# A decode attention kernel's SBUF places moved: first keys in the values' place, w1 and the second keys beside it, later query weights loaded mid-run

## The chip, the cores and the metric

The kernel runs on one core of a Trainium2 chip. The metric is the device time of one execution in microseconds. A difference of 0.3% (4 us) is about the least that can be told from no change here.

## What is computed

One decode step for eight sequences: a layer norm, then in parallel grouped-query attention over a cache of 8192 positions (32 query heads, 8 key/value heads of 128) and a dense layer with Mish; both are added to the input.

```python
xn = layernorm(x)                       # 8 x 512
q = (xn @ wq)                           # 32 heads x 128
scores = einsum("bhqd,bhkd->bhqk", q, repeat(k_cache, 4)) * 128 ** -0.5
o = einsum("bhqk,bhkd->bhqd", softmax(scores), repeat(v_cache, 4))
h = xn @ w1 + b1                        # 8 x 1792
act = h * tanh(softplus(h))
return x + o @ wo + act @ w2
```

All is float32. The caches are 268 MB each, so nearly all of the 561 MB that the kernel reads is keys and values, each read once.

## The kernel before

**Units.** The work is cut into 32 units, j = 0 to 31. Unit j holds batch b = j % 8 and the pair of key/value heads m = j // 8. Its keys are one load of 8.39 MB (128 partitions x 16384 floats, `ROW`) and its values another. wq is cut into four pairs of 2.10 MB (16 KB in each partition), one for each m; w1 is 3.67 MB, b1 is small.

**Places.** One SBUF tile, `kv`, takes every large load, as 2.5 x `ROW` columns. Even keys stand at 0, odd keys at `ROW // 2`: two units of keys share a half place. Values stand at 1.5 x `ROW` (`V_AT`). Before the loop the values' place holds three pairs of wq, then w1 (over the first two), b1 and the fourth pair; its spare part serves as scratch for Mish. x, its centred copy and its squares stand in the keys' place, at `ROW`.

**Queues.** The schedule is by hand: each engine executes its instructions in the order in which the program emits them, and the framework adds the waits. All large loads are issued by SyncE (`load_unit` L118, `load_pair` L111, w1 L425), in program order, each after its place has been read; x and b1 are issued by ScalarE. A load waits only for accesses to the columns that it overwrites.

**Before the loop.** x, three pairs of wq and keys 0 are issued. VectorE makes constants and the layer norm; `tr` (through its view `wide`) receives sixteen copies of the identity (L198). `project(m)` (L204 to L241) multiplies the normed x by the pair's weights (L209), copies it out on ScalarE (L217), transposes it through a matmul (L220), scales it into `qT` on VectorE (L228), and spreads it over the partitions with sixteen 128x128 selections taken from `wide` (L232, two halves, each copied by ScalarE into `qr`, L239). Each of these matmuls shows as two instructions in the profile. Projections 0, 1 and 2 run ahead of unit 0, projection 3 inside it.

**A unit.** `key_weights(j)` (L250, VectorE) expands the queries into block weights `wk`, of which there is one buffer. `scores` (L267, TensorE) multiplies them with the keys in two halves (`part`); the half that the next keys will overwrite is read first, and right after it SyncE issues the next keys. `softmax` (L279 to L300) is a short chain over VectorE, TensorE and ScalarE. `values(j - 1)` (L329) then reads the values of the unit before, after which SyncE issues the values of unit j into that place. `key_weights(j + 1)` follows on VectorE, and `turn(j)` transposes the probabilities: matmuls into X (L306), transposes into `tr` (L311) and reductions into `pt8` (L317), on VectorE. `merge(j - 1)` ends the unit. In unit 0 there are no values to read; in their place stand `mish` (L353 to L390, mostly a chain of VectorE steps that ends in the transpose into `aT`) and `project(3)`.

**The tail.** After the last unit the rows of wo and w2 are loaded into places that have come free, and the two output products are formed and added (L399, L411, L489).

Of the kernel before, what the change touches and what calls it, by code (L numbers as in the profile page):

```python
# [8 lines left out]
F32 = mybir.dt.float32  # L9
# [4 lines left out]
P = 128  # L14
B = 8
D = 512
HKV = 8
REP = 4
DH = 128
# [5 lines left out]
G = 4  # L25
NH = 2
TG = SK // (NH * G) // P
BW = 1024
CC = D // P
FG = F // G  # L30
FT = 4
FP = FG // FT
Q = P // G


NP = HKV // 2
NB = 2 * NH * G
ROW = NB * P * BW // P
DI = ROW // BW
# [11 lines left out]
W2R = 7  # L51


K_AT = (0, ROW // 2)
V_AT = ROW + ROW // 2
PLACES = V_AT + ROW


@with_exitstack
def kernel(  # L60
# [18 lines left out]
    ctx.enter_context(tc.manual_schedule())  # L79

    kv = const.tile([P, PLACES], F32, name="kv")

    S = psum.tile([P, 512], F32, name="s")
    X = psum.tile([P, 4, 512], F32, name="x4")
# [12 lines left out]
    gsel = const.tile([G, G, B], F32, name="gsel")  # L97
    xn4 = const.tile([P, CC, B], F32, name="xn4")
    xnT = const.tile([P, CC, B], F32, name="xnT")
    qr = const.tile([P, NP, DI, H2 * B], F32, name="qr")  # L100
    xres = const.tile([P, P], F32, name="xres")
    oT = const.tile([P, NP, H2, B], F32, name="oT")
    aT = const.tile([P, 2 * W2R, Q], F32, name="aT")
    pt8 = const.tile([P, HALF, PL * TL, H2], F32, name="pt8")
    tr = const.tile([P, PL * TL, 32], F32, name="tr")

    def load_pair(src, m, at):

        t = kv[:, at : at + 4096]
        rows = src.rearrange("j p f -> (j p f)").rearrange("(m p f) -> m p f", m=NP, p=P)  # L110
        nc.sync.dma_start(t, rows[m])  # L111
        return t

    def load_unit(src, j, at):
        m, b = divmod(j, B)
        lo = (b * HKV + 2 * m) * NH * G
        t = kv[:, at : at + ROW]
        nc.sync.dma_start(  # L118
            t,
            src[lo : lo + NB].rearrange("j p f -> (j p f)").rearrange("(p f) -> p f", p=P),  # L120
        )
        return t

    def load_k(j):
        return load_unit(kT, j, K_AT[j % 2])


    low = kv[:B, ROW : ROW + 3 * D]
    x_sb, xc, sq = (low[:, i * D : (i + 1) * D] for i in range(3))
    nc.scalar.dma_start(x_sb, x)  # L130
    wq_t = [load_pair(wq, m, V_AT + 4096 * m) for m in range(NP - 1)]
    k_t = {0: load_k(0)}


    make_identity(nc, ident)
# [51 lines left out]
    for g in range(G):  # L187
# [5 lines left out]
            stop=True,  # L193
        )
    nc.vector.tensor_copy(xres, M[:, 256:384])

    wide = tr.rearrange("p y c -> p (y c)")
    nc.vector.tensor_copy(  # L198
        wide.rearrange("p (o d) -> p o d", o=NB),
        ident.rearrange("p (o d) -> p o d", o=1).to_broadcast([P, NB, P]),  # L200
    )


    def project(m):  # L204

        w = wq_t[m].rearrange("p (c f) -> p c f", c=CC)
        for d in range(2):
            for c in range(CC):
                nc.tensor.matmul(  # L209
                    H[Q * c : Q * c + B, :],  # L210
                    xn4[:, c, :],
                    w[:, c, d * 512 : (d + 1) * 512],
                    start=True,
                    stop=True,
                )
            qp = work.tile([P, 512], F32, name="e")
            nc.scalar.copy(qp, H)  # L217
            for h in range(REP):
                at = 192 + (d * REP + h) * B
                nc.tensor.matmul(  # L220
                    M[:, at : at + B],
                    qp[:, h * DH : (h + 1) * DH],
                    bsel[:, :B],
                    start=True,
                    stop=True,
                )
        qT = work.tile([P, H2 * B], F32, name="qT")
        nc.vector.tensor_scalar_mul(qT, M[:, 192 : 192 + H2 * B], DH**-0.5)  # L228

        for half in range(2):  # L230
            for k in range(8):
                nc.tensor.matmul(  # L232
                    X[:, half, k * 64 : (k + 1) * 64],
                    wide[:, half * 8 + k :: DI],
                    qT,
                    start=True,
                    stop=True,
                )
            nc.scalar.copy(  # L239
                qr[:, m, half * 8 : (half + 1) * 8].rearrange("p i c -> p (i c)"), X[:, half]  # L240
            )  # L241

    WK = {}

    def key_weights(j):
        m, b = divmod(j, B)
        w = WK[j] = work.tile([P, DI, 2, NH * G, REP], F32, name="wk", bufs=1)
        q = qr[:, m].rearrange("p i (d o h b) -> p i d o h b", d=2, o=1, b=B)[..., b]
        for d in range(2):
            nc.vector.tensor_mul(  # L250
                w[:, :, d],
                q[:, :, d].to_broadcast([P, DI, NH * G, REP]),
                mask[:, d * NH * G : (d + 1) * NH * G]
                .rearrange("p (o k r) -> p o k r", o=1, r=1)
                .to_broadcast([P, DI, NH * G, REP]),
            )
# [20 lines left out]
    def softmax(j):  # L277
        nm = work.tile([P, 1], F32, name="nm")
        nc.vector.tensor_reduce(nm, S, axis=AX.X, op=ALU.max, negate=True)  # L279
        nc.tensor.transpose(M[:1, 0:P], nm, ident)  # L280
        nr = work.tile([1, 2, REP], F32, name="nr")
        row = M[:1, 0:P].rearrange("p (c d k h) -> p d h c k", c=2, d=2, h=REP)
        for d in range(2):
            nc.vector.tensor_reduce(nr[:, d], row[:, d], axis=AX.XY, op=ALU.min)
        nx = work.tile([1, 2, 2, NH * G, REP], F32, name="nx")
        for c in range(2):
            nc.vector.tensor_copy(  # L287
                nx[:, c],
                nr.rearrange("p d (o h) -> p d o h", o=1).to_broadcast([1, 2, NH * G, REP]),
            )  # L290
        nc.tensor.transpose(  # L291
            M[:, 128:129], nx.rearrange("p c d k h -> p (c d k h)"), ident[:1, :1]
        )
        nmx = work.tile([P, 1], F32, name="nmx")
        nc.vector.tensor_copy(nmx, M[:, 128:129])  # L295
        e = E[j] = work.tile([P, 512], F32, name="e")
        l = work.tile([P, 1], F32, name="l")
        nc.scalar.activation(e, S, AF.Exp, bias=nmx, accum_out=l)  # L298
        lsel = work.tile([P, H2], F32, name="lsel")
        nc.vector.tensor_scalar(lsel, rsel, l, None, op0=ALU.mult)  # L300
        return lsel
# [42 lines left out]
    def merge(j, os):  # L344
        m, b = divmod(j, B)
        nc.tensor.matmul(M[:, 168 : 168 + H2], os, hsel, start=True, stop=True)  # L346
        nc.vector.tensor_mul(oT[:, m, :, b], M[:, 168 : 168 + H2], RT.pop(j))


    def mish(w1_t, b1_sb, flat):  # L350
# [33 lines left out]
        for e in range(2):  # L384
# [2 lines left out]
                h[:, half * e : half * (e + 1)].rearrange("p (a l i) -> p a l i", a=2, i=W2R),  # L387
                t1[:, half * e : half * (e + 1)].rearrange("p (a l i) -> p a l i", a=2, i=W2R),
            )
        nc.vector.transpose(aT.rearrange("p j q -> p (j q)"), act)  # L390


    A = X[:, 0]
# [13 lines left out]
    def down(lo, hi, w):  # L407
        for j in range(2 * lo, 2 * hi):
            for g in range(G):
                at = (j - 2 * lo) * D + g * P  # L410
                nc.tensor.matmul(  # L411
                    H[Q * g : Q * g + B, :P],
                    aT[:, j, :B],
                    w[:, at : at + P],
                    start=(j == 0),
                    stop=(j == 2 * W2R - 1),
                )


    for m in range(NP - 1):  # L420
        project(m)
        if m == 0:
            key_weights(0)
    w1_t = kv[:, V_AT : V_AT + 7168].rearrange("p (j f) -> p j f", j=2 * CC)
    nc.sync.dma_start(w1_t, w1.rearrange("j p f -> p j f"))  # L425
    b1_sb = kv[:G, V_AT + 12288 - FG : V_AT + 12288]
    nc.scalar.dma_start(b1_sb, b1.rearrange("(g f) -> g f", g=G))
    wq_t.append(load_pair(wq, NP - 1, V_AT + 4096 * (NP - 1)))

    v_t = {}  # L430
    for j in range(UNITS):

        k = k_t.pop(j)
        scores(j, k, j % 2 == 1, 0)
        if j + 1 < UNITS:
            k_t[j + 1] = load_k(j + 1)
        else:
            v_t[j] = load_unit(v, j, 0)
        scores(j, k, j % 2 == 0, 1)
        WK.pop(j)  # L440
        lsel = softmax(j)
        os = None
        if j > 0:
            os = values(j - 1, v_t.pop(j - 1))
        else:
            mish(w1_t, b1_sb, kv[:, V_AT + 8192 : V_AT + 12288 - FG])
            project(NP - 1)
        if j + 1 < UNITS:
            v_t[j] = load_unit(v, j, V_AT)
            key_weights(j + 1)  # L450
        turn(j, lsel)
        if j > 0:
            merge(j - 1, os)


    w_o = [kv[:, V_AT + 4096 * m : V_AT + 4096 * (m + 1)] for m in range(NP)]
    for m in range(NP):
        nc.sync.dma_start(
            w_o[m].rearrange("p (u f) -> p u f", u=4),
# [3 lines left out]
    w2_t = []  # L463
    parts = ((0, 4), (4, 6), (6, 7))
    for lo, hi in parts:
        t = kv[:, ROW + lo * BW : ROW + hi * BW]
        nc.sync.dma_start(t, w2_rows[:, lo * BW : hi * BW])  # L467
        w2_t.append(t)

# [15 lines left out]
        )  # L485
    for p, t in zip(parts[1:], w2_t[1:]):
        down(*p, t)
    res = const.tile([P, P], F32, name="res")
    nc.vector.tensor_add(res, H[:, :P], xres)  # L489
    nc.sync.dma_start(out, res)  # L490

# [37 lines left out]
```

## Time and profile before

| | |
|---|---|
| time, median of 3 runs | 1344.5 us (1343.58 to 1347.8) |
| the profiled execution's own time | 1344.25 us |
| its span, first to last instruction | 1342.5 us |
| instructions | 11144 |
| TensorE busy, share of span | 999.7 us, 74% |
| VectorE busy | 508.4 us, 38% |
| ScalarE busy | 40.2 us, 3% |
| bytes moved, mean rate | 561.79 MB, 418 GB/s |
| mean granted TensorE clock | 0.875 |

In the profile's lines PE is TensorE (PEld its weight loads), DVE is VectorE, ACT is ScalarE, SP is SyncE; a q behind the name (SPq) is that engine's issuing of transfers. L267 is line 267 of the kernel before. `out<-in` names what an instruction writes and reads; x64 counts instructions merged into a row; a bracket tells how long the engine stood idle before it and what ended that. A row of the stages view holds the stage, its length, then for PE, PEld, DVE, ACT and POOL the busy time and the count, then the granted clock, the DMA share and GB/s. DMA shares in the slices are tenths.

### The profile page before, as it was taken

The page shows a single profiled execution, that of the slowest core. Times are in us where ns is not written, and L with a number is a line of the kernel's source. Part 1 is how long each engine was busy: PE and PEld are TensorE (multiplying, and loading weights), DVE is VectorE, ACT ScalarE, POOL GpSimd, SP SyncE. Part 2 cuts the span into 40 slices and gives each one's busy share as a digit, 9 for nine tenths or more (in the row PEclk, how much of TensorE's full clock was granted, in tenths as well). Part 3 has the DMA queues.
Part 4 walks back from the last instruction along what each step waited for, and adds up shares of the span by engine and source line. Part 5 has one row for each costly group of instructions (what it writes and reads, how often), then busy time and mean ns, then how long its engine had stood idle before and what let it go on. Part 6 is the DMA issues. An engine that isn't in the chain of part 4 may idle for free.

```text
span 1342.5 us, 11144 instructions
## 1 busy us (share of the span) xinstructions
PE 999.7 (74%) x5040; PEld 350.6 (26%) x5040; DVE 508.4 (38%) x724; ACT 40.2 (3%) x88; POOL 2.2 (0%) x9
## 2 busy tenths in 40 slices
PE   6879878677876776787676777777766887687676
PEld 4633222222222222222222222222222222222222
DVE  2043444443324444333344443244444224444431
ACT  1110000000000000000000000000000000000000
POOL 0000000000000000000000000000000000000000
PEclk9988888889988888888888789878888978887898
DMA  9569999999999999999999999999999999999997
GB/s 407 204 282 405 436 432 418 436 438 429 432 436 435 434 426 434 432 434 438 436 426 430 434 426 434 436 436 436 432 432 436 421 438 438 426 434 430 434 417 319
DMA packets 13591, 561.79 MB, mean 418 GB/s; under 512 B 1244, under 2 KB 1376, under 8 KB 4584
## 3 DMA queue, kind: packets, MB, share of 16 engines
q1 hardware_dynamic: 13520, 561.06, 97.1%
q8 instruction: 39, 0.64, 0.2%
q14 instruction: 8, 0.07, 0.0%
q10 hardware_dynamic: 24, 0.02, 0.0%
HBM read 561.01 MB, written 0.07 MB: 418 GB/s over the span
## 4 chain that ended last, share of the span: by engine, by line
DMA 70%; PE 26%; DVE 2%; SPq 2%; ACT 1%; issue 0%; ACTq 0%
DMA kv<-in_v 68%; PE o L329 19%; PE x L232 2%; PE s L267 2%; DMA kv<-in_w 2%; SPq L467 1%; PE m L220 1%; PE h L209 1%; PE x L306 0%; ACT e L217 0%; PE h L358 0%; ACT qr L239 0%; DVE kv L380 0%; DVE nm L279 0%; ACT L172 0%
## 5 line engine op out<-in xcount | busy, mean ns | idle before, releaser
L267 PE MATMUL s<-kv,wk 128*64 128x512 f32 x2048 | 512.0, 664 | 199.9 <-DMA kv<-in_kT 199.9
L329 PE MATMUL o<-kv,pt 128*32 128x512 f32 x2048 | 262.1, 670 | 49.7 <-DMA kv<-in_v 40.1
L267 PEld LDWEIGHTS s<-kv,wk 128*64 128x64 f32 x2048 | 157.2, 153 | 529.4 <-issue 326.6
L317 DVE TENSOR_REDUCE pt<-tr 64x512 f32<-64x2048 f32 x64 | 241.3, 3771 | 1.6
L279 DVE TENSOR_REDUCE nm<-s 128x1 f32<-128x512 f32 x32 | 22.1, 692 | 419.7 <-PE s L267 419.7
L329 PEld LDWEIGHTS o<-kv,pt 128*32 128x32 f32 x2048 | 68.9, 121 | 216.5 <-issue 164.1
L306 PE MATMUL x<-e,perm 128*128 128x512 f32 x256 | 121.3, 617 | 0.8 <-ACT qr L239 0.8
L337 DVE TENSOR_SCALAR os<-o,isel 128x128 f32<-128x128 f32 x32 | 11.2, 351 | 262.7 <-PE o L329 262.7
L311 DVE STREAM_TRANSPOSE tr<-x 128x512 f32<-128x512 f32 x128 | 78.6, 670 | 0.0
L306 PEld LDWEIGHTS x<-e,perm 128*128 128x128 f32 x256 | 47.1, 194 | 74.5 <-issue 74.5
L250 DVE TENSOR_TENSOR wk<-qr,mask 128x512 f32<-128x512 f32 x64 | 62.9, 1025 | 8.9 <-ACT qr L239 8.9
L298 ACT ACTIVATE e<-s,nmx 128x512 f32<-128x512 f32 x32 | 22.0, 687 | 1160.6 <-DVE nmx L295 1160.6
L232 PE MATMUL x<-qT,tr 128*128 128x64 f32 x128 | 29.9, 426 | 8.5 <-DVE qT L228 5.8
L339 DVE SCALAR_TENSOR_TENSOR os<-o,isel,os 128x128 f32<-128x128 f32 x96 | 33.7, 351 | 3.4
L232 PEld LDWEIGHTS x<-qT,tr 128*128 128x128 f32 x128 | 28.4, 309 | 9.6 <-DVE qT L228 6.1
L280 PE MATMUL m<-ident,nm 128*1 128x128 f32 x32 | 8.6, 270 | 25.5 <-DVE nm L279 25.5
L291 PE MATMUL m<-ident,nx 1*128 1x1 f32 x32 | 7.0, 217 | 24.2 <-DVE nx L287 24.2
L346 PE MATMUL m<-hsel,os 128*128 128x8 f32 x64 | 12.4, 266 | 9.3 <-DVE rt L309 9.3
L300 DVE TENSOR_SCALAR lsel<-rsel,l 128x8 f32<-128x8 f32 x32 | 7.4, 231 | 30.5 <-ACT e L298 30.5
L220 PE MATMUL m<-bsel,e 128*128 128x8 f32 x64 | 13.8, 344 | 6.0 <-ACT e L217 6.0
L220 PEld LDWEIGHTS m<-bsel,e 128*128 128x128 f32 x64 | 13.0, 301 | 18.5 <-ACT e L217 18.5
L280 PEld LDWEIGHTS m<-ident,nm 128*1 128x1 f32 x32 | 2.5, 79 | 53.7 <-DVE nm L279 53.7
(87 smaller groups left out, 156.7 us busy)
## 6 DMA issues: line engine op xcount, KB each, us to landing
kv<-in_wq SPq DMA_DIRECT2D x4, 2048.0 KB, 14.8
kv<-in_wo SPq DMA_DIRECT2D x4, 2048.0 KB, 29.3
kv<-in_w SPq DMA_DIRECT2D x1, 3584.0 KB, 13.5
kv<-in_w SPq DMA_DIRECT2D x1, 2048.0 KB, 37.1
kv<-in_w SPq DMA_DIRECT2D x1, 1024.0 KB, 20.7
kv<-in_kT SPq DMA_DIRECT2D x32, 29.4
kv<-in_v SPq DMA_DIRECT2D x32, 30.1
kv<-in_w SPq DMA_DIRECT2D x1, 512.0 KB
```

Source lines behind the costliest of these rows:

```text
L209: nc.tensor.matmul(H[Q * c : Q * c + B, :], xn4[:, c, :], w[:, c, d * 512 : (d + 1) * 512], start=True, stop=True,)
L220: nc.tensor.matmul(M[:, at : at + B], qp[:, h * DH : (h + 1) * DH], bsel[:, :B], start=True, stop=True,)
L232: nc.tensor.matmul(X[:, half, k * 64 : (k + 1) * 64], wide[:, half * 8 + k :: DI], qT, start=True, stop=True,)
L250: nc.vector.tensor_mul(w[:, :, d], q[:, :, d].to_broadcast([P, DI, NH * G, REP]), mask[:, d * NH * G : (d + 1) * NH * G] .rearrange("p (o ...
L267: nc.tensor.matmul(S[64 * c : 64 * (c + 1), :], w[:, i].rearrange("p d k h -> p (d k h)"), kk[:, i, c, :], start=(part == 0 and n == 0), s ...
L279: nc.vector.tensor_reduce(nm, S, axis=AX.X, op=ALU.max, negate=True)
L298: nc.scalar.activation(e, S, AF.Exp, bias=nmx, accum_out=l)
L306: nc.tensor.matmul(X[:, g], perm[:, g], e, start=True, stop=True)
L311: nc.vector.transpose(tr.rearrange("p (l t) c -> p t l c", t=TL)[:, tl], X.rearrange("p g (t q l) -> p t l g q", t=TL, q=PP)[:, tl],)
L317: nc.vector.tensor_reduce(pt8[half, :, :, d * REP : (d + 1) * REP].rearrange("p c y h -> p y c h"), tr[half].rearrange("p y (g c h) -> p y ...
L329: nc.tensor.matmul(O[Q * q : Q * (q + 1), :], pt8[:, c, TL * l : TL * (l + 1), :].rearrange("p t h -> p (t h)"), vt[:, 512 * n : 512 * (n ...
L339: nc.vector.scalar_tensor_tensor(os, O[:, DH * i : DH * (i + 1)], isel[:, i : i + 1], os, op0=ALU.mult, op1=ALU.add)
```

## The change

The values' place moves to the start of `kv`, and the two keys' places behind it. Keys 0 alone are loaded into the values' place; at the same time w1 and b1 stand in the even keys' place and keys 1 in the odd keys' place. One pair of wq has a place of its own, the new tile `ws`. Only pair 0 is loaded and projected ahead of the loop, and w1 and keys 1 are issued before that projection. `project` is split: `project` makes `qT`, `spread` makes `qr`, which now holds one pair instead of four. For the next pair, `load_q` is issued in the unit with b = 4 (behind that unit's values), `project` stands in the unit with b = 5 between `key_weights` and `turn`, and `spread` at the end of the unit with b = 6, after the identity copies have been written into `tr` again (`selections`), since `turn` overwrites `tr` in every unit. The copies now lie so that the weights of each spread matmul are contiguous, and are read from the identity with a stride. `aT` keeps only its 8 used columns of 32, through one more copy. A few tiles have one buffer less. The order inside `scores`, `softmax`, `values`, `turn` and `merge`, and the order of the tail, stay.

```diff
--- before.py
+++ after.py
@@ -51,9 +51,15 @@
 W2R = 7
-K_AT = (0, ROW // 2)
-V_AT = ROW + ROW // 2
-PLACES = V_AT + ROW
+V_AT = 0
+K_AT = (ROW, ROW + ROW // 2)
+W1_AT = ROW
+W2_AT = 2 * ROW
+PLACES = 2 * ROW + ROW // 2
+LOAD_Q, MAKE_Q, SPREAD_Q = 4, 5, 6
 @with_exitstack
@@ -79,6 +85,7 @@
     ctx.enter_context(tc.manual_schedule())
     kv = const.tile([P, PLACES], F32, name="kv")
+    ws = const.tile([P, CC * BW], F32, name="ws")
     S = psum.tile([P, 512], F32, name="s")
     X = psum.tile([P, 4, 512], F32, name="x4")
@@ -97,19 +104,17 @@
     gsel = const.tile([G, G, B], F32, name="gsel")
     xn4 = const.tile([P, CC, B], F32, name="xn4")
     xnT = const.tile([P, CC, B], F32, name="xnT")
-    qr = const.tile([P, NP, DI, H2 * B], F32, name="qr")
+    qr = const.tile([P, DI, H2 * B], F32, name="qr")
     xres = const.tile([P, P], F32, name="xres")
     oT = const.tile([P, NP, H2, B], F32, name="oT")
-    aT = const.tile([P, 2 * W2R, Q], F32, name="aT")
+    aT = const.tile([P, 2 * W2R, B], F32, name="aT")
     pt8 = const.tile([P, HALF, PL * TL, H2], F32, name="pt8")
     tr = const.tile([P, PL * TL, 32], F32, name="tr")
-    def load_pair(src, m, at):
-        t = kv[:, at : at + 4096]
-        rows = src.rearrange("j p f -> (j p f)").rearrange("(m p f) -> m p f", m=NP, p=P)
-        nc.sync.dma_start(t, rows[m])
-        return t
+    def load_q(m):
+        rows = wq.rearrange("j p f -> (j p f)").rearrange("(m p f) -> m p f", m=NP, p=P)
+        nc.sync.dma_start(ws, rows[m])
     def load_unit(src, j, at):
         m, b = divmod(j, B)
@@ -121,15 +126,15 @@
         )
         return t
-    def load_k(j):
-        return load_unit(kT, j, K_AT[j % 2])
-    low = kv[:B, ROW : ROW + 3 * D]
+    low = kv[:B, W1_AT : W1_AT + 3 * D]
     x_sb, xc, sq = (low[:, i * D : (i + 1) * D] for i in range(3))
     nc.scalar.dma_start(x_sb, x)
-    wq_t = [load_pair(wq, m, V_AT + 4096 * m) for m in range(NP - 1)]
-    k_t = {0: load_k(0)}
+    b1_sb = kv[:G, W1_AT + 7168 : W1_AT + 7168 + FG]
+    nc.scalar.dma_start(b1_sb, b1.rearrange("(g f) -> g f", g=G))
+    load_q(0)
+    k_t = {0: load_unit(kT, 0, V_AT)}
+    w1_t = kv[:, W1_AT : W1_AT + 7168].rearrange("p (j f) -> p j f", j=2 * CC)
     make_identity(nc, ident)
@@ -193,17 +198,21 @@
             stop=True,
         )
     nc.vector.tensor_copy(xres, M[:, 256:384])
-    wide = tr.rearrange("p y c -> p (y c)")
-    nc.vector.tensor_copy(
-        wide.rearrange("p (o d) -> p o d", o=NB),
-        ident.rearrange("p (o d) -> p o d", o=1).to_broadcast([P, NB, P]),
-    )
-    def project(m):
-        w = wq_t[m].rearrange("p (c f) -> p c f", c=CC)
+    wide = tr.rearrange("p y c -> p (y c)").rearrange("p (i o) -> p i o", i=DI)
+    def selections():
+        nc.vector.tensor_copy(
+            wide.rearrange("p i (x g) -> p i x g", x=NB),
+            ident.rearrange("p (o g i) -> p i o g", o=1, i=DI).to_broadcast([P, DI, NB, DG]),
+        )
+    selections()
+    def project():
+        w = ws.rearrange("p (c f) -> p c f", c=CC)
         for d in range(2):
             for c in range(CC):
                 nc.tensor.matmul(
@@ -224,28 +233,31 @@
                     start=True,
                     stop=True,
                 )
-        qT = work.tile([P, H2 * B], F32, name="qT")
+        qT = work.tile([P, H2 * B], F32, name="qT", bufs=1)
         nc.vector.tensor_scalar_mul(qT, M[:, 192 : 192 + H2 * B], DH**-0.5)
+        return qT
+    def spread(qT):
         for half in range(2):
             for k in range(8):
                 nc.tensor.matmul(
                     X[:, half, k * 64 : (k + 1) * 64],
-                    wide[:, half * 8 + k :: DI],
+                    wide[:, half * 8 + k],
                     qT,
                     start=True,
                     stop=True,
                 )
             nc.scalar.copy(
-                qr[:, m, half * 8 : (half + 1) * 8].rearrange("p i c -> p (i c)"), X[:, half]
+                qr[:, half * 8 : (half + 1) * 8].rearrange("p i c -> p (i c)"), X[:, half]
             )
     WK = {}
     def key_weights(j):
-        m, b = divmod(j, B)
+        b = j % B
         w = WK[j] = work.tile([P, DI, 2, NH * G, REP], F32, name="wk", bufs=1)
-        q = qr[:, m].rearrange("p i (d o h b) -> p i d o h b", d=2, o=1, b=B)[..., b]
+        q = qr.rearrange("p i (d o h b) -> p i d o h b", d=2, o=1, b=B)[..., b]
         for d in range(2):
             nc.vector.tensor_mul(
                 w[:, :, d],
@@ -282,7 +294,7 @@
         row = M[:1, 0:P].rearrange("p (c d k h) -> p d h c k", c=2, d=2, h=REP)
         for d in range(2):
             nc.vector.tensor_reduce(nr[:, d], row[:, d], axis=AX.XY, op=ALU.min)
-        nx = work.tile([1, 2, 2, NH * G, REP], F32, name="nx")
+        nx = work.tile([1, 2, 2, NH * G, REP], F32, name="nx", bufs=1)
         for c in range(2):
             nc.vector.tensor_copy(
                 nx[:, c],
@@ -387,7 +399,9 @@
                 h[:, half * e : half * (e + 1)].rearrange("p (a l i) -> p a l i", a=2, i=W2R),
                 t1[:, half * e : half * (e + 1)].rearrange("p (a l i) -> p a l i", a=2, i=W2R),
             )
-        nc.vector.transpose(aT.rearrange("p j q -> p (j q)"), act)
+        turned = flat[:, 5 * FG : 6 * FG]
+        nc.vector.transpose(turned, act)
+        nc.vector.tensor_copy(aT, turned.rearrange("p (j q) -> p j q", q=Q)[:, :, :B])
     A = X[:, 0]
@@ -410,32 +424,30 @@
                 at = (j - 2 * lo) * D + g * P
                 nc.tensor.matmul(
                     H[Q * g : Q * g + B, :P],
-                    aT[:, j, :B],
+                    aT[:, j, :],
                     w[:, at : at + P],
                     start=(j == 0),
                     stop=(j == 2 * W2R - 1),
                 )
-    for m in range(NP - 1):
-        project(m)
-        if m == 0:
-            key_weights(0)
-    w1_t = kv[:, V_AT : V_AT + 7168].rearrange("p (j f) -> p j f", j=2 * CC)
     nc.sync.dma_start(w1_t, w1.rearrange("j p f -> p j f"))
-    b1_sb = kv[:G, V_AT + 12288 - FG : V_AT + 12288]
-    nc.scalar.dma_start(b1_sb, b1.rearrange("(g f) -> g f", g=G))
-    wq_t.append(load_pair(wq, NP - 1, V_AT + 4096 * (NP - 1)))
+    k_t[1] = load_unit(kT, 1, K_AT[1])
+    qT = project()
+    spread(qT)
+    key_weights(0)
     v_t = {}
     for j in range(UNITS):
+        b = j % B
+        more = j // B + 1 < NP
         k = k_t.pop(j)
         scores(j, k, j % 2 == 1, 0)
-        if j + 1 < UNITS:
-            k_t[j + 1] = load_k(j + 1)
-        else:
-            v_t[j] = load_unit(v, j, 0)
+        if j == UNITS - 1:
+            v_t[j] = load_unit(v, j, K_AT[0])
+        elif j > 0:
+            k_t[j + 1] = load_unit(kT, j + 1, K_AT[(j + 1) % 2])
         scores(j, k, j % 2 == 0, 1)
         WK.pop(j)
         lsel = softmax(j)
@@ -443,17 +455,23 @@
         if j > 0:
             os = values(j - 1, v_t.pop(j - 1))
         else:
-            mish(w1_t, b1_sb, kv[:, V_AT + 8192 : V_AT + 12288 - FG])
-            project(NP - 1)
+            mish(w1_t, b1_sb, kv[:, W1_AT : W1_AT + 6 * FG])
         if j + 1 < UNITS:
             v_t[j] = load_unit(v, j, V_AT)
             key_weights(j + 1)
+        if more and b == LOAD_Q:
+            load_q(j // B + 1)
+        if more and b == MAKE_Q:
+            qT = project()
         turn(j, lsel)
         if j > 0:
             merge(j - 1, os)
-    w_o = [kv[:, V_AT + 4096 * m : V_AT + 4096 * (m + 1)] for m in range(NP)]
+        if more and b == SPREAD_Q:
+            selections()
+            spread(qT)
+    w_o = [kv[:, 4096 * m : 4096 * (m + 1)] for m in range(NP)]
     for m in range(NP):
         nc.sync.dma_start(
             w_o[m].rearrange("p (u f) -> p u f", u=4),
@@ -463,7 +481,7 @@
     w2_t = []
     parts = ((0, 4), (4, 6), (6, 7))
     for lo, hi in parts:
-        t = kv[:, ROW + lo * BW : ROW + hi * BW]
+        t = kv[:, W2_AT + lo * BW : W2_AT + hi * BW]
         nc.sync.dma_start(t, w2_rows[:, lo * BW : hi * BW])
         w2_t.append(t)
@@ -485,7 +503,7 @@
         )
     for p, t in zip(parts[1:], w2_t[1:]):
         down(*p, t)
-    res = const.tile([P, P], F32, name="res")
+    res = work.tile([P, DH], F32, name="os")
     nc.vector.tensor_add(res, H[:, :P], xres)
     nc.sync.dma_start(out, res)
```

## The prediction

> **What bounds the kernel now.** Keys and values come from HBM once, so I read the transfer rate first, by slices on the page, then by stages (busy time of each engine with its count; the last three columns are granted TensorE clock, DMA share and GB/s).
>
> ```profile
> DMA  9569999999999999999999999999999999999997
> GB/s 407 204 282 405 436 432 418 436 438 429 432 436 435 434 426 434 432 434 438 436 426 430 434 426 434 436 436 436 432 432 436 421 438 438 426 434 430 434 417 319
> ```
> ```profile
> 0.00:140.00 140.00, 110.67 (x530) 61.16 (x530) 40.20 (x85) 16.24 (x27) 2.20 (x9) 0.93 0.78 327
> 140.00:1300.00 1160.00, 864.80 (x4254) 281.37 (x4255) 456.07 (x627) 23.36 (x60) 0.00 (x0) 0.87 1.00 433
> 1300.00:1342.50 42.50, 24.22 (x258) 8.09 (x256) 12.16 (x14) 0.59 (x1) 0.00 (x0) 0.84 0.81 331
> ```
> ```profile
> 0.00:5.00 5.00, 0.00 (x0) 0.00 (x0) 3.95 (x19) 1.28 (x1) 2.20 (x9) 1.00 0.67 216
> ```
>
> From 140 to 1300 us the DMA engines are full at 433 GB/s, with TensorE 75% and VectorE 39% busy: a microsecond there is bought only with fewer bytes or lost with an empty queue. The loss is at the front: the first 140 us move 327 instead of 433 GB/s, which is 140 x (1 - 327/433) = 34.3 us of transfer time; 2.5 of it (5 x (1 - 216/433)) is the start that any order has. That leaves **31.8 us of holes**. The tail's loss is there too, but the change leaves its order as it is. SyncE's issues say where the holes lie (start, us to issue):
>
> ```profile
> 0.74 1.33 SPq L111 DMA_DIRECT2D kv<-in_wq  x3
> 2.11 0.68 SPq L118 DMA_DIRECT2D kv<-in_kT  x1
> 35.13 0.38 SPq L425 DMA_DIRECT2D kv<-in_w  x1
> 35.55 0.58 SPq L111 DMA_DIRECT2D kv<-in_wq  x1
> 72.56 0.33 SPq L118 DMA_DIRECT2D kv<-in_kT  x1
> 96.88 0.33 SPq L118 DMA_DIRECT2D kv<-in_v  x1
> 119.62 0.33 SPq L118 DMA_DIRECT2D kv<-in_kT  x1
> ```
> ```profile
> 73.50:74.00 0.50, 0.50 (x4) 0.14 (x2) 0.00 (x0) 0.00 (x0) 0.00 (x0) 1.00 5.60 1835
> ```
>
> A unit of keys or values (8.39 MB) takes 19.4 us at 433 GB/s, a pair of wq (2.10 MB) 4.85, w1 (3.67 MB) 8.5. An issue into an empty queue moves its first packets about 1.2 us later (72.56 to about 73.8). So w1 and the last wq end near 50 and nothing moves until 73.8; keys 1 end at 93.2 and values 0 start at 98.1; they end at 117.5 and keys 2 start at 120.8: 24 + 5 + 3 us, the 31.8 again. The next views give the steady loop, which decides what a late issue costs.
>
> ```profile
> 441.68 0.33 SPq L118 DMA_DIRECT2D kv<-in_v  x1
> 448.02 7.55 DVE L317 TENSOR_REDUCE pt<-tr 64x512 f32<-64x2048 f32 x2
> 453.90 16.89 PE L267 MATMUL s<-kv,wk 128*64 128x512 f32 x64 [7.84 <-DMA kv<-in_kT]
> 463.97 0.33 SPq L118 DMA_DIRECT2D kv<-in_kT  x1
> ```
> ```profile
> 434.54 7.12 PE o L329 x64
> 441.68 31.54 DMA kv<-in_v
> 473.26 8.81 PE o L329 x64
> 482.09 29.86 DMA kv<-in_v
> ```
>
> Keys land at 453.9 and the next are issued 10.1 us later, when the first half of the scores has read the shared half place; values land at 473.3, 19.4 after the keys, so the keys queue 9.3 us ahead of need. **A unit may start its scores up to 8 us late (9.3 - 1.2) before the queue runs empty.** The reductions of `turn` end at 455.57, 13.9 us after the values' issue: 1.7 us after the next keys land, or 3.4 where `values` takes 8.8 instead of 7.1. I take 2.8.
>
> **The change, part by part.** *The front.* Before keys 0 only wq of pair 0 is loaded; w1 and keys 1 follow. Rows of before:
>
> ```profile
> 10.91 0.61 PE L188 MATMUL m<-kv,ident 8*8 8x128 f32 x8 [0.38 <-DVE xnT L186]
> 11.79 1.22 DVE L198 COPY tr<-ident 128x2048 f32<-128x2048 f32 x1
> 20.65 3.73 PE L232 MATMUL x<-qT,tr 128*128 128x64 f32 x16 [0.32 <-DVE qT L228]
> 25.05 3.74 PE L232 MATMUL x<-qT,tr 128*128 128x64 f32 x16 [0.68 <-ACT qr L239]
> 29.45 1.96 DVE L250 TENSOR_TENSOR wk<-qr,mask 128x512 f32<-128x512 f32 x2 [8.85 <-ACT qr L239]
> 63.51 15.83 PE L267 MATMUL s<-kv,wk 128*64 128x512 f32 x64
> 79.39 0.69 DVE L279 TENSOR_REDUCE nm<-s 128x1 f32<-128x512 f32 x1 [24.01 <-PE s L267]
> 96.16 0.65 DVE L390 STREAM_TRANSPOSE aT<-kv 128x448 f32<-128x448 f32 x1
> 96.84 1.94 DVE L250 TENSOR_TENSOR wk<-qr,mask 128x512 f32<-128x512 f32 x2
> ```
>
> The new w1 place holds x and its normalised copy, so w1 waits on SyncE for L188, until 11.5; only keys 1 stand behind it, and wq 0 with keys 0 keep the queue full until 2 + 24.2 = 26.2. w1 and keys 1 follow without a hole, to 54.1. TensorE now goes from pair 0's projection straight to the scores: the weights are there at 31.4 as before, keys 0 landed at 26, so scores 0 run 31.5 to 47.3 (15.83) instead of from 63.5. Their end frees the values' place; values 0 are issued at 47.4, 5.5 us before they are needed, and move from 54.1 to 73.5. This closes the holes of 24 and 5 us.
>
> What is late next: the weights for scores 1 are made on VectorE behind the Mish chain. In before they are done at 98.78, 19.4 us after the scores' end at 79.34; the new copy of aT adds some 0.3 (bounds 0.2 and 0.6, a small copy and the transpose above). So scores 1 start at 47.3 + 19.7 = 67.0, their first half takes 9 (63.51 to 72.56) to 10.1 us, keys 2 are issued at 76.5 and move from 77.7. **One hole of 4.2, say 4.5 us, stays.** Values 0 pass late enough that nothing behind opens: scores 1 end near 84, `values` near 94, and keys 2 last until 97.1. The b1 load joins x's on ScalarE's queue at the start, where ScalarE has nothing to do until VectorE has x's mean: nothing.
>
> *Mid-run weights, three times.* Each load stands behind values 4 of its pair on SyncE, its place long free: no wait. The 3 x 4.85 us of transfer are moved from the front, no byte is added; keys 6 land 4.85 later behind it. One unit on, `project` stands on TensorE between `values` and `turn`:
>
> ```profile
> 86.11 1.04 PE L209 MATMUL h<-kv,xn 128*8 128x512 f32 x8 [0.75 <-DVE kv L366]
> 90.71 1.44 PE L220 MATMUL m<-bsel,e 128*128 128x8 f32 x8 [0.76 <-ACT e L217]
> ```
>
> 86.11 to 92.15 is 6.0 us; at the pace of the first 20 us (11.5 to 20.4) 9. Behind it wait `turn`, the scores, and on VectorE the qT product and the transposes. The cover is TensorE's wait for keys, 7.8 us above, plus the 4.85 of this very load: 12.7, so nothing; without that load the excess over 8 us would show.
>
> *The spread, three times.* This is the exposed step. It needs `tr` and X free, so its copy stands on VectorE behind `turn`'s reductions, which end 2.8 us after keys 7 landed; TensorE waits for it, with scores 7 queued behind. The copy reads its source with a stride, which no row shows: not under 1.22 (same size, unstrided), not over 3.8 (a reduction reading 2048 with strides):
>
> ```profile
> L317 DVE TENSOR_REDUCE pt<-tr 64x512 f32<-64x2048 f32 x64 | 241.3, 3771 | 1.6
> ```
>
> I take 1.3, next to the same copy. The spread takes 20.65 to 28.79 = 8.15. Its weights are now contiguous. I count nothing for that: by the rows
>
> ```profile
> 14.05 1.88 PE L220 MATMUL m<-bsel,e 128*128 128x8 f32 x8 [0.70 <-ACT e L217]
> ...
> 87.92 1.06 PE L220 MATMUL m<-bsel,e 128*128 128x8 f32 x8 [0.76 <-ACT e L217]
> ```
>
> contiguous loads of that size ran at the spread's own pace of 0.23 us in the same stretch. At the second row's 0.13 us the whole would take about 5. So scores 7 start 2.8 + 1.3 + 0.1 + 8.15 = 12.3 us late. In before the first spread block that ran straight into scores gave 9.0 to the next keys' issue. Keys 8 issue at 21.3, move at 22.5; values 6 ended at 19.4: **a hole of 3.1 us, 9.4 in three.** Both ends: 1.7 + 1.2 + 5 + 7.1 + 1.2 = 16.2, no hole; 3.4 + 3.8 + 8.2 + 10.1 + 1.2 = 26.7, a hole of 7.3. Behind it `values` 6 end 25 us after scores 7 started, at 37.3, while keys 8 last to 41.9: no second hole.
>
> *Sum.* 31.8 - 4.5 - 9.4 = 17.9 us less. The profiled execution took 1344.25 (span 1342.5 and 1.75 around it), beside a median of 1344.5: **1326 us**.
>
> **The clock, trace and skill.** What the hole turns on is TensorE's pace after a wait.
>
> ```profile
> 63.50:68.00 4.50, 4.50 (x13) 1.39 (x14) 0.00 (x0) 0.59 (x1) 0.00 (x0) 1.00 0.00 2
> 96.90:105.20 8.30, 7.46 (x32) 7.09 (x32) 1.88 (x3) 0.64 (x2) 0.00 (x0) 0.50 0.95 379
> ```
> ```profile
> 112.56 13.91 PE s L267 x64
> ```
>
> The spread of 96.9 to 105.2 was granted half the clock for its whole 8.3 us, busy as it was; scores right after a spread did 13 matmuls in their first 4.5 us (0.35 each, then 0.22), while those at 112.56, after dense work, ran 0.217 from the start. The Trainium skill, "TensorE: Matmul & The Clock Gate", Part 1, says that some 3.4 us of sustained matmuls release the full clock; by that the spread's second half and the scores behind it would run at full pace. The trace disagrees for this block. It stays a rival.
>
> **Rivals.** (1) *The spread warms TensorE.* Second half 2.1 instead of 3.74, first half of the scores 7.1 instead of 9.0: keys 8 move at 19.0, before values 6 end, and only the first hole stays: 1344.25 - 31.8 + 4.5 = **1317**. For: dense matmuls do recover within 4.5 us. Against: the half clock above, and both halves at 3.7 in every spread of before. (2) *Slower: TensorE stays at half pace into scores 7.* Their first half then takes 32 x 0.434 = 13.9, and with the copy at 3.8 and the late reductions the keys move at 3.4 + 3.8 + 0.1 + 8.2 + 13.9 + 1.2 = 30.6: 11.2 us in each of three pairs, 38.1 with the first hole, 6 more than is won: **1350**. It decides from 9.1 us a pair ((31.8 - 4.5)/3). For: the granted 0.50. Against: 63.51, where scores behind a spread sped up within 4.5 us. (3) *The front is not filled:* if w1 (and keys 1 behind it) were held until keys 0 are read, at 47.4, the queue would stand empty from 26.2 to 48.6, 22.4 us; the hole before keys 2 goes, and with the spreads' 9.4 nothing is won: **1344**. Against: the kernel before already loads beside live parts of the same tile, keys into a half place.
>
> **The numbers.** Forecast 0.66 (1320 to 1338: holes of 1 to 7 us a pair), rival 1 0.22, rival 2 0.07, rival 3 0.05. The range 1313 to 1338 covers the first two and leaves out some 0.15. A measurement here can tell 0.3%, 4 us, from no change: faster 0.88, same 0.05, slower 0.07.
>
> **What would show it.** Keys 1 issued near 12, scores 0 from 31.5, values 0 issued near 47.4, and no empty DMA before 73; keys 2 issued at 76 to 77. After that three dips only, some 3 us each, near 316, 634 and 952, each behind a block of L232's kind that ends 12 us after keys landed, with the keys' issue 9 us later. A dip behind `project`, or one ahead of the values that follow, would show a step wrong; so would a steady rate other than 433 GB/s, on which all sums rest.

## The result and the profile after

The changed kernel takes **1329.46 us** (median of five; 1328.93 to 1336.04) against 1344.51 before (five; 1343.58 to 1347.8): ratio 0.990, 95% interval 0.987 to 0.993. The profiled execution took 1329.46 with a span of 1327.7. Forecast were 1326 and a range of 1313 to 1338.

The rate by slices and by stages of the changed kernel, as read before (last three columns of a stage: granted clock, DMA share, GB/s):

```profile
DMA  9999999998999999999999999999899999999998
GB/s 394 443 407 418 439 440 418 439 435 340 431 439 441 417 433 439 435 433 427 393 433 423 435 439 431 431 429 439 370 417 435 439 437 423 432 439 437 429 414 334
```
```profile
0.00:140.00 140.00, 98.72 (x486) 38.88 (x488) 64.31 (x108) 10.03 (x17) 2.20 (x9) 0.92 0.98 416
140.00:1290.00 1150.00, 869.24 (x4306) 302.66 (x4302) 440.62 (x612) 29.62 (x70) 0.00 (x0) 0.87 0.99 427
1290.00:1327.70 37.70, 22.37 (x250) 7.87 (x250) 9.88 (x10) 0.59 (x1) 0.00 (x0) 0.77 0.83 335
```

The front runs at 416 GB/s instead of 327. The long stretch is at 427 instead of 433, and three slices (340, 393, 370) hold that loss. Landings give the exact account: the first matmul row that waited for a load starts when it landed. The rows are those for values 1 and for keys 31 in the kernel before, the changed kernel, and the best version (experiment 6), which serves as the measure for a front without holes:

```profile
162.09 8.77 PE L329 MATMUL o<-kv,pt 128*32 128x512 f32 x64 [1.84 <-DMA kv<-in_v]
...
1271.26 16.11 PE L267 MATMUL s<-kv,wk 128*64 128x512 f32 x64 [6.25 <-DMA kv<-in_kT]
```
```profile
118.26 8.58 PE L341 MATMUL o<-kv,pt 128*32 128x512 f32 x64 [3.02 <-DMA kv<-in_v]
...
1254.63 15.60 PE L279 MATMUL s<-kv,wk 128*64 128x512 f32 x64 [7.99 <-DMA kv<-in_kT]
```
```profile
115.70 8.77 PE L341 MATMUL o<-kv,pt 128*32 128x512 f32 x64 [0.36 <-DMA kv<-in_v]
...
1239.51 15.40 PE L279 MATMUL s<-kv,wk 128*64 128x512 f32 x64 [7.83 <-DMA kv<-in_kT]
```

Before values 1 the kernel before also loaded three pairs of wq, 14.5 us: its front lost 162.1 - 14.5 - 115.7 = 31.9 us to holes, the 31.8 of the rates. The changed kernel's front loses 2.6. From there to keys 31 it takes 1136.4 us, the best version with the same loads 1123.8: **12.6 us are given back mid-run.** That makes 31.9 - 2.6 - 12.6 = 16.7, and the keys 31 do land 16.6 earlier; the tail behind them is 1.8 us longer (73.1 instead of 71.2). The spans differ by 14.8. The 1123.8 is also what the kernel before takes for the same stretch (1271.26 - 162.09 = 1109.2) with three query loads of 4.85 us added.

SyncE's issues and the steps of the front, by the two timelines:

```profile
11.64 0.38 SPq L434 DMA_DIRECT2D kv<-in_w  x1
12.07 8.05 SPq L123 DMA_DIRECT2D kv<-in_kT  x1
47.63 0.33 SPq L123 DMA_DIRECT2D kv<-in_v  x1
75.80 0.33 SPq L123 DMA_DIRECT2D kv<-in_kT  x1
```
```profile
31.33 16.26 PE L279 MATMUL s<-kv,wk 128*64 128x512 f32 x64 [2.64 <-DVE wk L262]
65.28 1.92 DVE L262 TENSOR_TENSOR wk<-qr,mask 128x512 f32<-128x512 f32 x2
67.25 15.37 PE L279 MATMUL s<-kv,wk 128*64 128x512 f32 x64 [9.88 <-DVE wk L262]
```

Each stands within a microsecond of its forecast (11.5, 31.5, 47.4, 67.0, 76.5). The first mid-run spread, in the timeline around 310 us (L329 the reductions of `turn`, L205 the copies, L244 the spread, L279 the scores):

```profile
293.47 7.55 DVE L329 TENSOR_REDUCE pt<-tr 64x512 f32<-64x2048 f32 x2
...
301.13 1.88 DVE L205 COPY tr<-ident 128x2048 f32<-128x2048 f32 x1
303.07 3.67 PE L244 MATMUL x<-qT,tr 128*128 128x64 f32 x16 [11.56 <-DVE tr L205]
...
307.41 3.68 PE L244 MATMUL x<-qT,tr 128*128 128x64 f32 x16 [0.68 <-ACT qr L251]
311.02 16.36 PE L279 MATMUL s<-kv,wk 128*64 128x512 f32 x64
...
320.56 0.33 SPq L123 DMA_DIRECT2D kv<-in_kT  x1
```

The chain is the forecast one: TensorE stands 11.6 us for the copies, the spread runs at half pace in both halves (granted clock 0.50), and the scores behind it start without a wait for keys. Keys 6 and 8 show in rows of the same kernel, and behind them the same steps at the other two places (keys 14 land, keys 16 are issued and land; keys 22, then keys 24):

```profile
258.94 16.80 PE L279 MATMUL s<-kv,wk 128*64 128x512 f32 x64 [2.67 <-DMA kv<-in_kT]
...
343.69 15.39 PE L279 MATMUL s<-kv,wk 128*64 128x512 f32 x64 [2.83 <-DMA kv<-in_kT]
```
```profile
580.99 16.20 PE L279 MATMUL s<-kv,wk 128*64 128x512 f32 x64 [3.98 <-DMA kv<-in_kT]
...
639.47 0.33 SPq L123 DMA_DIRECT2D kv<-in_kT  x1
...
662.56 13.95 PE L279 MATMUL s<-kv,wk 128*64 128x512 f32 x64 [2.79 <-DMA kv<-in_kT]
...
899.91 15.46 PE L279 MATMUL s<-kv,wk 128*64 128x512 f32 x64 [2.29 <-DMA kv<-in_kT]
...
960.20 0.33 SPq L123 DMA_DIRECT2D kv<-in_kT  x1
...
982.11 13.95 PE L279 MATMUL s<-kv,wk 128*64 128x512 f32 x64 [1.60 <-DMA kv<-in_kT]
```

A load of 8.39 MB lands every 19.35 us in this stretch, so a unit takes 38.7. By that, keys 7 landed at 297.7, values 6 at 317.0, and keys 8 were due at 336.3. They were issued at 320.6 and landed 7.3 us late. In the other two places it is 4.2 and 4.8 us.

### The profile page after: what moved, and what is told of

It reads as the page before. It is cut to its first block, busy times and chain, and to the rows that moved or that the text cites. A ratio compares the mean times of both kernels' runs of the same rounds, so it can differ in the third digit from the quotient of the medians.

```text
span 1327.7 us, 11151 instructions
## 1 busy us (share of the span) xinstructions
PE 990.3 (75%) x5040; PEld 349.4 (26%) x5040; DVE 514.8 (39%) x728; ACT 40.2 (3%) x88; POOL 2.2 (0%) x9
## 4 chain that ended last, share of the span: by engine, by line
DMA 65%; PE 29%; DVE 5%; ACT 1%; issue 0%; SPq 0%
DMA kv<-in_v 62%; PE o L341 19%; PE s L279 6%; DMA kv<-in_w 3%; PE x L244 2%; DVE pt L329 2%; PE x L318 1%; DVE tr L323 1%; DVE tr L205 0%; PE h L425 0%; DVE wk L262 0%; PE m L229 0%; PE h L218 0%; DVE nm L291 0%; PE h L370 0%
## 5 line engine op out<-in xcount | busy, mean ns | idle before, releaser
L279 PE MATMUL s<-kv,wk 128*64 128x512 f32 x2048 | 507.4, 659 | 165.7 <-DMA kv<-in_kT 153.1
L341 PE MATMUL o<-kv,pt 128*32 128x512 f32 x2048 | 258.5, 663 | 51.8 <-DMA kv<-in_v 42.2
L279 PEld LDWEIGHTS s<-kv,wk 128*64 128x64 f32 x2048 | 156.3, 152 | 491.6 <-issue 322.9
L329 DVE TENSOR_REDUCE pt<-tr 64x512 f32<-64x2048 f32 x64 | 241.4, 3771 | 1.6
L318 PE MATMUL x<-e,perm 128*128 128x512 f32 x256 | 126.7, 641 | 0.0
L244 PE MATMUL x<-qT,tr 128*128 128x64 f32 x128 | 29.4, 424 | 37.7 <-DVE tr L205 34.7
L244 PEld LDWEIGHTS x<-qT,tr 128*128 128x128 f32 x128 | 27.9, 330 | 38.8 <-DVE tr L205 35.0
L321 DVE RECIPROCAL rt<-m 128x8 f32<-128x8 f32 x32 | 6.6, 207 | 29.7 <-PE m L319 29.7
## 6 DMA issues: line engine op xcount, KB each, us to landing
kv<-in_w SPq DMA_DIRECT2D x1, 1024.0 KB, 20.7
```

What stands on the lines that cost most here:

```text
L244: nc.tensor.matmul(X[:, half, k * 64 : (k + 1) * 64], wide[:, half * 8 + k], qT, start=True, stop=True,)
L279: nc.tensor.matmul(S[64 * c : 64 * (c + 1), :], w[:, i].rearrange("p d k h -> p (d k h)"), kk[:, i, c, :], start=(part == 0 and n == 0), s ...
L318: nc.tensor.matmul(X[:, g], perm[:, g], e, start=True, stop=True)
L329: nc.vector.tensor_reduce(pt8[half, :, :, d * REP : (d + 1) * REP].rearrange("p c y h -> p y c h"), tr[half].rearrange("p y (g c h) -> p y ...
L341: nc.tensor.matmul(O[Q * q : Q * (q + 1), :], pt8[:, c, TL * l : TL * (l + 1), :].rearrange("p t h -> p (t h)"), vt[:, 512 * n : 512 * (n ...
```

## The experiments

The theory: the front is won because transfers fill the queue while unit 0 computes, and part of it is given back in three places, because the next keys' issue hangs on scores that are queued behind copies and spread. Rival A: the mid-run loss is the work itself (loads, projections, VectorE's or TensorE's time). Rival B: a wait moved to the values. All runs changed one thing in the changed kernel, unless the diff says otherwise.

**1. The block moved behind the first half of the next scores** and the keys' issue.

```diff
+        if more and b == SPREAD_Q + 1:
+            selections()
+            spread(qT)
         scores(j, k, j % 2 == 0, 1)
...
-        if more and b == SPREAD_Q:
-            selections()
-            spread(qT)
```

> The identity copies and the spread move from the end of the unit with b = 6 to behind the first half of the next unit's scores; nothing else. Theory (the three mid-run holes, some 15.9 us together, exist because the next scores, and with them the next keys' issue, are queued behind the spread): the keys are issued about 10 us after the keys before them landed again, the values' issue some 8 us later than usual stays ahead of need, all three holes go, 1313.5 us (1312 to 1317). Rival A (the loss is the mid-run work itself: the query loads, the projection, TensorE's time): 1327 to 1331, as with the change. Rival B (the wait is only handed to the values): half comes back, about 1321.

Measured: 1317.43 us (five; 1316.94 to 1319.54), ratio to before 0.981 (0.979 to 0.982), 0.4 above the theory's range. Its stage over the first spread, that place in its timeline, and the landings of values 1 and keys 31:

```profile
290.00:360.00 70.00, 53.46 (x262) 19.67 (x263) 29.11 (x38) 2.73 (x6) 0.00 (x0) 0.85 1.00 433
```
```profile
298.83 8.46 PE L279 MATMUL s<-kv,wk 128*64 128x512 f32 x32 [7.83 <-DMA kv<-in_kT]
...
300.63 1.89 DVE L205 COPY tr<-ident 128x2048 f32<-128x2048 f32 x1
307.22 2.00 PE L244 MATMUL x<-qT,tr 128*128 128x64 f32 x16
307.34 0.33 SPq L123 DMA_DIRECT2D kv<-in_kT  x1
...
309.90 2.00 PE L244 MATMUL x<-qT,tr 128*128 128x64 f32 x16 [0.68 <-ACT qr L251]
311.82 8.78 PE L279 MATMUL s<-kv,wk 128*64 128x512 f32 x32
```
```profile
119.78 9.22 PE L341 MATMUL o<-kv,pt 128*32 128x512 f32 x64 [4.92 <-DMA kv<-in_v]
...
1243.62 15.68 PE L279 MATMUL s<-kv,wk 128*64 128x512 f32 x64 [7.84 <-DMA kv<-in_kT]
```

The keys are issued 8.5 us after the keys before landed, the copies run beside the scores, and the stage is back at 433 GB/s, where the changed kernel's has 389. Rivals A and B fall: from values 1 to keys 31 this kernel takes 1123.8 us, as the best version does, so the same work in another place costs nothing and all of the 12.6 is back. The time is 12.0 less and not the 15.9 that I had expected from the stretch's mean rate: against 433 GB/s the best version slips some microseconds there too. In the profiled executions the front is 1.5 us longer here than in the changed kernel, and the tail 1.1 shorter.

**2. No mid-run spread.**

```diff
         if more and b == SPREAD_Q:
             selections()
-            spread(qT)
```

> The mid-run spread is left out (pairs 1 to 3 use the queries of pair 0, so the output is not the reference's); the query loads, the projections and the identity copies stay where they were. Theory: nothing stands ahead of the next scores any more, the copies on VectorE are waited for by nobody: 1313.5 us (1312 to 1317), no dip near 316, 634 and 952. Rival A (loads or projection are what costs): stays at 1327 to 1331.

Measured: 1319.38 and 1318.84 us, above the theory's range, yet without dips in the long stretch:

```profile
290.00:360.00 70.00, 52.52 (x236) 17.47 (x236) 32.39 (x43) 1.56 (x4) 0.00 (x0) 0.85 1.00 433
```

The excess is in the front: its first 100 us run at 394 GB/s instead of the changed kernel's 415, with keys 2 issued at 79.1 instead of 75.8. Values 1 land at 121.5, 5.8 us after the best version's 115.7; from there to keys 31 it is 1123.8 us once more. Why the front varies is the subject of the last section, and experiment 6 closes its hole.

**3. Copies without a stride.** The layout and the strided weight reads of the kernel before.

> The identity copies lie as in the kernel before: copied without a stride, the spread's weights read with one. Theory (every part of the chain in front of the scores counts, one for one): the copy takes 1.22 instead of 1.88 us, the spread 0.2 more, three times 0.5 less: 1328 us, at the edge of what can be told; the copy's row must show 1.2 us and the holes 0.5 us less each. Rival (strided weights load slower once the stage is cold): the spread's blocks over 3.74 us each and no gain, 1329.5 or more.

Measured: 1327.72 to 1330.56 us in four executions, median 1329.75: no difference that can be told. The groups by line show both terms as expected (1.22 us a copy instead of 1.88, and 29.9 instead of 29.4 us in all spreads), but the 0.5 us a pair doesn't reach the time. By landings, too, values 1 to keys 31 take 1136.3 us, against 1136.4 in the changed kernel. The keys are issued 21.0, 21.3 and 21.4 us after the landing before them, together 0.6 less than there, not 1.5. So the theory's one for one isn't confirmed at this size, and the rival's blocks of over 3.74 us aren't there either (29.9 us are 3.74 a block): what took up the rest is not shown.

```profile
L244 PE MATMUL x<-qT,tr 128*128 128x64 f32 x128 | 29.9, 425 | 35.7 <-DVE tr L205 32.7 <-ACT qr L251 2.7 <-DVE qT L237 0.3
...
L205 DVE COPY tr<-ident 128x2048 f32<-128x2048 f32 x4 | 4.9, 1218 | 0.0
```

**4. Three copies instead of one**, in the changed kernel's place and behind the first half of the scores.

```diff
-            selections()
+            for _ in range(3):
+                selections()
             spread(qT)
```

> The changed kernel with the identity copies written three times mid-run instead of once: 2 x 1.88 us more on VectorE ahead of each spread, where it stands in the changed kernel. Theory (the chain in front of the next scores is exposed one for one): three holes 3.8 us longer each, 1340.7 us (1338 to 1343). Rival (VectorE, busy 39% of the time, has room for it): 1329 to 1331.

> The same three copies, with the block behind the first half of the next scores. Theory (there the copies run while the scores' first half runs, and nothing that issues keys waits for them): 1317.4 us as with one copy (1316 to 1320). Rival (VectorE's added time counts wherever it stands): 1325 or more.

Measured in the changed kernel's place: 1344.86 us (ten; 1341.72 to 1346.07), ratio to before 0.999 (0.998 to 1.000): the whole gain is gone. Behind the first half of the scores: 1317.8 us (four; 1316.09 to 1319.38), as with one copy. In the timeline of the first:

```profile
304.49 5.71 DVE L205 COPY tr<-ident 128x2048 f32<-128x2048 f32 x3
...
318.21 16.37 PE L279 MATMUL s<-kv,wk 128*64 128x512 f32 x64
...
327.76 0.33 SPq L123 DMA_DIRECT2D kv<-in_kT  x1
```

The lowest execution, 1341.72, is 12.8 us above the changed kernel's lowest, for 11.5 us of copies: one for one and a little more. By landings it is the same: values 1 to keys 31 take 12.8 us more than in the changed kernel. The median lies above the range; the profiled execution, 1346.04, issued keys 2 at 79.5 and so has some 3 us from the front in it. The same VectorE time costs nothing where no keys' issue hangs on it.

**5. The order of two issues in the front:** keys 1 behind values 0 instead of behind w1.

```diff
 v_t[j] = load_unit(v, j, V_AT)
+if j == 0:
+    k_t[1] = load_unit(kT, 1, K_AT[1])
```

> Only the order of two issues: keys 1 are issued behind values 0 (which wait for scores 0) instead of behind w1. Theory (the front's gain is transfers that fill the queue while unit 0 computes): the queue is empty from about 34.7 to 48.8, keys 1 land near 87.6 and keys 2 are issued near 97, after 10.6 empty us instead of 3; with 14.1 + 7.6 more, 1351 us (1347 to 1354), which gives the whole front back. Rival (the front's gain is TensorE's, one projection ahead of scores 0 instead of three): 1329 to 1333.

Measured: 1352.68 and 1354.71 us, ratio 1.007 (1.005 to 1.009). Scores 1 stand 32 us for keys 1 (the second row merges two issues, keys 1 at 47.75 and keys 2 at 98.5):

```profile
47.36 0.34 SPq L123 DMA_DIRECT2D kv<-in_v  x1
47.75 51.11 SPq L123 DMA_DIRECT2D kv<-in_kT  x2
...
89.40 15.97 PE L279 MATMUL s<-kv,wk 128*64 128x512 f32 x64 [32.30 <-DMA kv<-in_kT]
...
140.96 8.77 PE L341 MATMUL o<-kv,pt 128*32 128x512 f32 x64 [2.90 <-DMA kv<-in_v]
```

TensorE's share of the front (one projection ahead of the scores instead of three) is still there, yet values 1 land at 140.96 instead of 118.26. So 22.7 of the front's 29.3 us (31.9 - 2.6) are lost, where 21.7 were expected: most of the front's gain is the filled queue. The other 6.6 us stay; the time still ends above before's because the mid-run loss is paid here too.

**6. Unit 1's key weights ahead of Mish**, together with experiment 1.

```diff
+            key_weights(1)
             mish(w1_t, b1_sb, kv[:, W1_AT : W1_AT + 6 * FG])
         if j + 1 < UNITS:
             v_t[j] = load_unit(v, j, V_AT)
-            key_weights(j + 1)
+            if j > 0:
+                key_weights(j + 1)
```

> The spread behind the first half of the scores as before, and unit 1's key weights made ahead of Mish on VectorE instead of behind it. Theory (the hole that stays in front is there because scores 1 wait 10 us for weights that stand behind the Mish chain): scores 1 start near 54 when keys 1 land, keys 2 are issued near 66, when Mish has left its scratch, ahead of the end of values 0 at 73.8; the hole of some 5 us goes: 1312.5 us (1310.5 to 1315). Rival (the transposes of unit 0, now behind Mish too late for values 0, hold values 1 instead): 1316 to 1319.

Measured: **1313.26 us** (four; 1313.04 to 1313.54), ratio to before 0.977 (0.975 to 0.978), the best version of all.

```profile
51.23 1.96 DVE L262 TENSOR_TENSOR wk<-qr,mask 128x512 f32<-128x512 f32 x2
57.73 13.95 PE L279 MATMUL s<-kv,wk 128*64 128x512 f32 x64 [1.29 <-DVE kv L387]
...
64.88 0.33 SPq L123 DMA_DIRECT2D kv<-in_kT  x1
```
```profile
0.00:100.00 100.00, 71.78 (x348) 31.13 (x350) 49.25 (x87) 9.24 (x15) 2.20 (x9) 0.94 1.00 424
```

Keys 2 are issued at 64.9, twelve microseconds ahead of the landing of values 0 (counted back from values 1 at 19.35 a load: 115.7 - 38.7 = 77.0). Scores 1 start at 57.7 and not near 54; by the same count keys 1 land only then (57.65). The scatter is smallest here: 0.5 us, against 2.6 and 3.3 with the front's hole alone (experiment 1 and the second kernel of 4) and 2.8 to 7.1 with all four holes (experiment 3 and the changed kernel). That a hole hands on what TensorE's clock does (last section), and that a full queue hides it, fits these few executions and isn't shown by them.

**7. The next pair's load two units earlier.** `LOAD_Q` 2 instead of 4.

> The changed kernel with the next pair's load issued in the unit with b = 2 instead of 4, so that its 4.85 us no longer lie in front of the unit that projects. Theory (the projection's 6 us fit into the 8 us by which scores may start late, with or without the load beside them): 1329.5 us (1327 to 1332). Rival (the projection is hidden only by its own load): scores of the unit after start 2 us late and more is lost in three places, 1334 or more.

Measured: 1336.5 us (four: 1331.69, 1336.26, 1336.75, 1337.11), ratio 0.993 (0.992 to 0.995), by its median the rival's side. But the rival's mechanism isn't there: in the profiled execution (1337.11) the scores behind a projection start within a microsecond of their keys. Its front issued keys 2 at 79.0, like experiment 2, and values 1 land 3.4 us later than in the changed kernel's profiled execution. From there to keys 31 it takes 4.6 us more: the keys are issued 22.2, 23.5 and 23.0 us after the landing before them, there 22.9, 19.8 and 21.6. The second hole shows where that can come from:

```profile
602.79 9.13 PE L341 MATMUL o<-kv,pt 128*32 128x512 f32 x64 [3.36 <-DMA kv<-in_v]
```

Without the load's delay TensorE goes from projection to scores at full pace, ends them early and waits longer for the values (3.4 us instead of 1.1). It reads them at a granted clock of 0.77, in 9.1 us where the changed kernel has 1.00 and 7.1, ahead of `turn`, copies and spread. So the load may help in its place, through the clock. That is read from one execution and not shown: the wait alone does not set the pace, since a wait of 0.5 us in the changed kernel (values 5, at 278.29) went with 8.8.

## Why the prediction was right, and where it was off

- **The bound, and the front's gain:** right. 31.8 us of holes were there to win by the forecast, 31.9 by landings; the best version is 31.4 us below before (1344.7 - 1313.26), and experiment 5 loses 22.7 of the front's 29.3 again through a queue that stands empty.
- **The hole before keys 2** (4.5 us, behind the Mish chain): right in place; 2.6 in the profiled execution, 5.8 in that of experiment 2, where the clock is lower. Experiment 6 closes it, 4.2 us between the medians of 1 and 6.
- **Loads and projections mid-run at nothing:** right where they stand; experiment 1 keeps both and takes 1123.8 us from values 1 to keys 31, as the kernel before does with the loads added.
- **The spread, 3.1 us a pair:** the mechanism is right (1, 2, 4), and so is the chain: the keys are issued 22.9, 19.8 and 21.6 us after the keys before them landed, 21.3 were forecast. Within it the copy took 1.88 instead of 1.3 (I had taken the unstrided row); the scores started 13.4, 11.7 and 13.4 us late (12.3 forecast), and their first half took 9.5, 8.1 and 8.2 (9.0 forecast), so that the chain comes out right in the mean, by terms that miss both ways. **What failed is the step "an issue into an empty queue moves its first packets about 1.2 us later".** First packets are not the price. Keys issued into an empty queue landed 23.1 (320.56 to 343.69), 23.1 and 21.9 us after their issue, and 21.9 in the front (75.80, row below), against 19.35 between landings in a full queue: a restart costs 2.5 to 3.8 us. With it the three holes come to 7.3 + 4.2 + 4.8 = 16.3 instead of 9.4 us; 12.6 of it is net, since the best version, too, slips 6.3 us over that stretch (1123.8 against 57 loads of 19.35 and three of 4.85), and this one 2.6 beside its holes. The first place shows why first packets mislead:

```profile
314.50:321.50 7.00, 7.00 (x32) 2.29 (x30) 0.00 (x0) 0.00 (x0) 0.00 (x0) 0.90 0.00 0
```

For these 7.0 us no packet of a load starts, although values 6 count as landed only at 317.0: their last packets had started by 314.1, and those of keys 8 begin at 321.5, 1.0 us after the issue. The forecast set the start of one transfer against the landing of the other (22.5 and 19.4 us after keys 7 landed), and here the landing came 2.9 us after the start of the last packets. This is read from the first place alone. The restart in the front is this row:

```profile
97.67 15.52 PE L279 MATMUL s<-kv,wk 128*64 128x512 f32 x64 [1.56 <-DMA kv<-in_kT]
```

- **Sum:** 31.8 - 4.5 - 9.4 = 17.9 forecast; 31.9 - 2.6 - 12.6 = 16.7 measured up to keys 31, and 1.8 of a longer tail, which was forecast to stay. 1.3 of the 1.8 is there when values 30 land, 20.7 us after keys 31 (1275.32) against 19.35 before (1290.61); why they land later stays open.
- **Rival 1** (a warm spread, 1317) is out by the rows: 3.67 and 3.68 in the two halves. **Rival 2** is out by the first halves of the scores behind the spread: 9.5, 8.1 and 8.2 us, where it needed 13.9. **Rival 3** is out by the issue at 12.07; experiment 5, which holds back keys 1 alone, shows what such a wait costs.

## What to carry to other kernels

Where transfers are the bound, price a moved step by what its queue position does to the next load's issue, not by its engine's idle share: here the same block, three times, cost 12.6 us ahead of the matmuls that release a buffer, and nothing behind them. Count how late a load may be issued before its queue runs empty, add up the chain in front of it, and price a restart by issue-to-landing against the cadence of a full queue (here 2.5 to 3.8 us), not by its first packets.

## What was not expected of the hardware

**The clock at the front varies, and a hole makes it visible.** Keys 2 were issued at 75.8 to 79.5 us in the profiled executions of kernels with the same front. The rows that differ are Mish's first product (L370) and what follows; here the changed kernel with copies tripled, whose front is unchanged:

```profile
51.10 6.04 PE L370 MATMUL h<-kv,xnT 128*8 128x448 f32 x32
...
79.46 0.33 SPq L123 DMA_DIRECT2D kv<-in_kT  x1
```

The same product took 3.19 us at a granted clock of 1.00 where keys 2 were issued at 75.8, 4.61 at 0.68 in experiment 7, and 6.04 at 0.52 here. The scores behind add to it: in experiment 1 the product took 3.19 again, but the first half of scores 1 ran at 0.70 instead of 0.83, and keys 2 were issued at 77.0. The five executions of the changed kernel lie at 1329 (three) and at 1334 and 1336. Of the changed kernel itself only a lower one was profiled; that its upper ones come from the clock in such places is argued, not shown.

**The spread kept the pace that it met.** It took 3.67 us a half, at a granted clock of 0.50, after an idle TensorE, and 2.00, at 1.00, when dense scores ran just before (experiment 1). The Trainium skill, "TensorE: Matmul & The Clock Gate", Part 1, has the full clock return after some 3.4 us of sustained matmuls. In these traces 8 us of 128x64 products with a 128x128 weight load each did not bring it back; the dense scores behind them had it after some 5 us (0.50 from 311.0 to 315.5, 1.00 from 316.0).
